# wo in 32 contiguous rows per partition, and head outputs spread by a masked multiply, in a one-core attention block

## The chip, the cores and the metric

The kernel runs on one core of a Trainium2 chip. The metric is the device time of one execution in microseconds. A run over 1.5% above the fastest of its kernel is called slow and is left out of every ratio. Times of one set were taken on the same chip, in turns with the kernel before.

In the profiles, PE is TensorE (PEld its weight loads), DVE is VectorE, ACT is ScalarE, POOL is GpSimd and SP is SyncE, which issues the loads. HBM is the memory in which the inputs stand, SBUF the memory of the core, in 128 partitions. A packet is one piece that a DMA moves, here one run of bytes of a partition; a DMA has landed when its last completion signal is recorded. The granted clock is the share of full speed that the trace gives for TensorE.

## The reference

One decode step: a grouped-query attention over a long cache, times a gate from a small MLP. The attention is cut to what matters here; `xn` is the layer-normed input.

```python
B, Sq, D = 2, 1, 512
Hq, Hkv, Sk, Dh = 32, 8, 32768, 128        # 4 query heads share a KV head
q = (xn @ wq)                              # [B, 32 heads, 128]
scores = einsum("bhqd,bhkd->bhqk", q, k) * Dh**-0.5
o = einsum("bhqk,bhkd->bhqd", softmax(scores), v)
s = o.reshape(B, Sq, Hq * Dh) @ wo         # wo is [4096, 512]
out = x + s * silu(mlp(xn))
```

K and V together are 268 MB. wo is 4 MB and is used last.

## The kernel before

K and V come in 4 MB pieces (one DMA each, 32 KB to every partition) into five buffers that are used in turn. They stand in the pool `slots`, which is laid out behind `pers`, the pool of everything that lives for the whole kernel.

```python
pers = ctx.enter_context(tc.tile_pool(name="pers", bufs=1))
slots = ctx.enter_context(tc.tile_pool(name="slots", bufs=SLOTS))     # 5 x 32 KB per partition
ktp = ctx.enter_context(tc.tile_pool(name="ktp", bufs=T_BUFS))        # transposed keys
# ... other work pools, and PSUM pools
def load_cache(cache, b, g, i, name):
    t = slot(name)
    nc.sync.dma_start(out=t[:, :],
        in_=cache[b, g, i * NK:(i + 1) * NK, :].rearrange("(p t) d -> p (t d)", p=128))
    return t
# ... the parts of pers that the change touches
sel_r = pers.tile([128, NQ, 4, 32], BF16)      # 1024 bytes per partition, filled by 4 copies
mask = pers.tile([128, NQ, rep], F32)          # 64 bytes, filled by 4 reduces
oX = pers.tile([128, Hkv, NQ, B], BF16)
```

At the end of each KV head the head's output is divided by the softmax sum and moved to the partitions where the wo rows lie. Then the last three DMAs, wo, feed 128 output matmuls.

```python
    # end of a head (b, g)
    on = smp.tile([128, rep], BF16, tag="on", name="on")
    nc.vector.tensor_mul(out=on[:, :], in0=oT[:, :], in1=rec[:, :])
    for r in range(NQ):
        nc.tensor.matmul(xp[:, r, :], lhsT=sel_r[:, r, :, :]..., rhs=on[:, :], start=True, stop=True)
    nc.vector.tensor_mul(out=xm[:, :, :], in0=xp[:, :, :], in1=mask[:, :, :])
    nc.vector.tensor_reduce(out=oX[:, g, :, b], in_=xm[:, :, :], axis=AX.X, op=ALU.add)

wo_parts = [(0, 4), (4, 7), (7, 8)]            # of 8 groups, 4 KB per partition each
# ... in the last round, queued behind the last V piece
for a, z in wo_parts:
    nc.sync.dma_start(out=wo3[:, a:z, :], in_=wos[:, a:z, :])
# ... after the loop
for gr in range(Hkv * NQ):
    g, r = divmod(gr, NQ)
    for n in range(NQ):
        c = r * D + n * QW
        nc.tensor.matmul(s_ps[32 * n:32 * n + B, :], lhsT=oX[:, g, r, :], rhs=wo3[:, g, c:c + QW],
                         start=(gr == 0), stop=(gr == Hkv * NQ - 1), tile_position=(0, 32 * n))
# sg = s_ps * g4; out4 = sg + x4; two stores of 1 KB, one by SP, one by ACT
```

The softmax here doesn't subtract the row's maximum and nothing guards it: scores larger than these inputs give would overflow.

## Time and profile before

| what | value | where it is read |
|---|---|---|
| time | 661.57 us | median of 3 runs, 661.44 to 661.58 |
| profiled span | 660.0 us | page |
| bytes moved, mean rate | 280.91 MB, 426 GB/s | page, part 2 |
| PE, DVE busy | 63%, 53% | page, part 1 |
| 32,768 B load packet | 1213 ns (median) | packet records of the trace |
| slowest of the 16 landings of the last wo part | 655.51 us | landing records of the trace |

The page of the kernel before. In part 2 each number is one fortieth of the span; part 4 is the chain of waits followed back from the end; in part 6 the last number is the time from issue to landing.

```profile
span 660.0 us, 6356 instructions
PE 415.5 (63%) x2684; PEld 175.7 (27%) x2684; DVE 347.9 (53%) x442; ACT 50.1 (8%) x152; POOL 6.9 (1%) x20
...
DMA  9999999999999999999999999999999999999995
GB/s 382 419 437 442 418 438 439 424 439 425 434 436 427 439 428 429 440 427 434 437 425 437 432 429 440 425 434 439 427 435 428 435 436 427 437 434 429 432 419 232
...
q1 hardware_dynamic: 10728, 280.50, 98.7%
q8 instruction: 21, 0.34, 0.2%
...
DMA k<-in_A_k_cache_dram 70%; PE sc L304 10%; DVE T L296 7%; DMA wo<-in_A_wo_dram 6%; PE o L336 3%; DVE pt L315 1%; ACT ep L313 0%; PE S L332 0%; PE s_ps L394 0%; DVE sm L331 0%; SPq L93 0%; SPq L380 0%; DVE sg L402 0%; DVE out L404 0%; DVE
...
k<-in_A_k_cache_dram SPq DMA_DIRECT2D x32, 4096.0 KB, 44.9
```

The DMA engines are busy from the first slice to the last, at 418 to 442 GB/s in all slices but the first and the last, and most of the chain is K loads (70%) and wo (6%). A K load lands 44.9 us after its issue, which at 426 GB/s is the time of 4.6 loads of 4.19 MB (an estimate from these numbers), so others are queued ahead of it: the engines do not wait for the core. So the time is the bytes at the rate of the DMA packets, plus what follows the last landing.

The timeline of the end of the kernel before (start, length, engine, line, operation; in brackets the idle time before it and what ended it):

```profile
650.80 0.16 DVE L355 TENSOR_TENSOR on<-oT,rec 128x4 bf16<-128x4 f32 x1 [11.72 <-PE oT L348]
651.02 0.24 PE L358 MATMUL xp<-on,sel_r 128*128 128x4 bf16 x4 [0.25 <-DVE on L355]
651.19 1.06 PE L394 MATMUL s_ps<-wo,oX 128*2 128x128 bf16 x64
651.30 0.17 DVE L363 TENSOR_TENSOR xm<-xp,mask 128x16 f32<-128x16 f32 x1 [0.33 <-PE xp L358]
651.50 0.17 DVE L365 TENSOR_REDUCE oX<-xm 128x4 bf16<-128x16 f32 x1
654.33 1.88 PE L394 MATMUL s_ps<-wo,oX 128*2 128x128 bf16 x64 [2.08 <-DMA wo<-in_A_wo_dram]
656.26 0.29 DVE L402 TENSOR_TENSOR sg<-s_ps,g 98x128 f32<-98x128 f32 x1 [4.58 <-PE s_ps L394]
656.65 0.29 DVE L404 TENSOR_TENSOR out<-sg,x 98x128 bf16<-98x128 f32 x1
656.97 0.65 SPq L406 DMA_DIRECT2D out_dram<-out  x1
```

PE waits 2.08 us for the second wo part, then 64 matmuls fill the time to 656.21. The rest is one multiply, one add and the store.

### The profile page before, as it was taken

To read this page: it belongs to the slowest core of one execution; us is meant where nothing else is said; L and a number is where in the kernel's file an instruction comes from. 1 tells how busy PE (TensorE), PEld (TensorE's weight loads), DVE (VectorE), ACT (ScalarE), POOL (GpSimd) and SP (SyncE) were. 2 spreads that over 40 slices of the span, in tenths; PEclk is the share of its full clock that TensorE was granted. 3 is DMA by queue.
4 is the path that set the end of the run, shared out by engine and by line. 5 is a ranking of instruction groups with operands and counts; after the bars stand their busy time and mean duration, and the time that the engine had idled before them with its cause. 6 is when DMAs were issued, how large, how long until landed. Compare 5 with 4: busy or idle time off the path is not lost.

```text
span 660.0 us, 6356 instructions
## 1 busy us (share of the span) xinstructions
PE 415.5 (63%) x2684; PEld 175.7 (27%) x2684; DVE 347.9 (53%) x442; ACT 50.1 (8%) x152; POOL 6.9 (1%) x20
## 2 busy tenths in 40 slices
PE   2485667565566766467776566766646775656664
PEld 2242223222222322223222122322212232222222
DVE  5563456564445655445656444665644466554450
ACT  1111100000000000000000000000000000000000
POOL 3000000000000000000000000000000000000000
PEclk9985897676888767678777777877778787768886
DMA  9999999999999999999999999999999999999995
GB/s 382 419 437 442 418 438 439 424 439 425 434 436 427 439 428 429 440 427 434 437 425 437 432 429 440 425 434 439 427 435 428 435 436 427 437 434 429 432 419 232
DMA packets 11024, 280.91 MB, mean 426 GB/s; under 512 B 1386, under 2 KB 1396, under 8 KB 2420
## 3 DMA queue, kind: packets, MB, share of 16 engines
q1 hardware_dynamic: 10728, 280.50, 98.7%
q8 instruction: 21, 0.34, 0.2%
q0 software_dynamic: 256, 0.01, 0.0%
q14 instruction: 7, 0.06, 0.0%
q10 hardware_dynamic: 12, 0.00, 0.0%
HBM read 280.50 MB, written 0.00 MB: 425 GB/s over the span
## 4 chain that ended last, share of the span: by engine, by line
DMA 75%; PE 14%; DVE 7%; issue 2%; ACT 0%; SPq 0%; DVEq 0%; ACTq 0%
DMA k<-in_A_k_cache_dram 70%; PE sc L304 10%; DVE T L296 7%; DMA wo<-in_A_wo_dram 6%; PE o L336 3%; DVE pt L315 1%; ACT ep L313 0%; PE S L332 0%; PE s_ps L394 0%; DVE sm L331 0%; SPq L93 0%; SPq L380 0%; DVE sg L402 0%; DVE out L404 0%; DVEq L296 0%
## 5 line engine op out<-in xcount | busy, mean ns | idle before, releaser
L304 PE MATMUL sc<-T,z 128*128 128x512 bf16 x1024 | 301.1, 461 | 179.7 <-DVE T L296 179.5
L296 DVE STREAM_TRANSPOSE T<-k 128x1024 int32<-128x1024 int32 x256 | 292.1, 1207 | 167.7 <-DMA k<-in_A_k_cache_dram 167.7
L304 PEld LDWEIGHTS <-z 128*128 128x128 bf16 x1024 | 114.7, 112 | 365.1 <-issue 283.8
L336 PE MATMUL o<-v,pt 128*16 128x512 bf16 x1024 | 73.8, 439 | 4.9 <-DMA v<-in_A_v_cache_dram 4.9
L315 DVE STREAM_TRANSPOSE pt<-ep 128x512 bf16<-128x512 bf16 x32 | 22.8, 711 | 78.1 <-ACT ep L313 78.1
L313 ACT ACTIVATE ep<-sc 128x512 bf16<-128x512 f32 x32 | 19.1, 597 | 533.5 <-PE sc L304 533.5
L336 PEld LDWEIGHTS <-pt 128*16 128x16 bf16 x1024 | 25.4, 97 | 41.1 <-issue 23.7
L332 PE MATMUL S<-sm,ones_f 128*128 128x4 f32 x64 | 12.1, 260 | 24.8 <-DVE sm L331 24.8
L348 PE MATMUL oT<-sel_o,ob 128*128 128x4 f32 x128 | 16.9, 255 | 11.1 <-ACT ob L345 11.1
L348 PEld LDWEIGHTS oT<-sel_o,ob 128*128 128x128 f32 x128 | 15.5, 191 | 19.4 <-ACT ob L345 19.4
L332 PEld LDWEIGHTS S<-sm,ones_f 128*128 128x128 f32 x64 | 9.7, 191 | 32.5 <-DVE sm L331 32.5
L327 DVE MEMSET o<- 128x512 f32 x16 | 7.8, 485 | 13.4 <-ACT ob L345 12.3
L280 ACT COPY z<-qr 32x16 bf16<-32x16 bf16 x64 | 12.7, 198 | 11.6 <-DVE qr L227 10.9
L355 DVE TENSOR_TENSOR on<-oT,rec 128x4 bf16<-128x4 f32 x16 | 2.6, 161 | 20.2 <-PE oT L348 20.2
L345 ACT COPY ob<-o 128x512 f32<-128x512 f32 x16 | 9.4, 584 | 26.2 <-PE o L336 26.2
L353 DVE RECIPROCAL rec<-S 128x4 f32<-128x4 f32 x16 | 2.9, 182 | 7.3 <-PE S L332 7.2
L358 PEld LDWEIGHTS <-sel_r 128*128 128x128 bf16 x64 | 5.2, 117 | 5.2 <-issue 5.2
L209 PE MATMUL qT_ps<-xT,wq 128*128 128x2 bf16 x128 | 3.6, 165 | 4.5 <-DMA wq<-in_A_wq_dram 4.5
L358 PE MATMUL xp<-on,sel_r 128*128 128x4 bf16 x64 | 3.8, 164 | 4.0 <-DVE on L355 4.0
L313 ACT ACTIVATION_READ_ACCUMULATOR ep<-sc 128x1 f32 x32 | 6.3, 198 | 0.2
L331 DVE TENSOR_SCALAR sm<-sel_h,rs 128x4 f32<-128x4 f32 x32 | 6.0, 188 | 0.0
L363 DVE TENSOR_TENSOR xm<-xp,mask 128x16 f32<-128x16 f32 x16 | 2.8, 174 | 5.3 <-PE xp L358 5.3
(63 smaller groups left out, 48.5 us busy)
## 6 DMA issues: line engine op xcount, KB each, us to landing
k<-in_A_k_cache_dram SPq DMA_DIRECT2D x32, 4096.0 KB, 44.9
v<-in_A_v_cache_dram SPq DMA_DIRECT2D x32, 4096.0 KB, 39.2
wq<-in_A_wq_dram SPq DMA_DIRECT2D x1, 4096.0 KB, 12.5
w<-in_B_w_dram SPq DMA_DIRECT2D x2, 1792.0 KB, 38.0
wo<-in_A_wo_dram SPq DMA_DIRECT2D x1, 2048.0 KB, 34.4
wo<-in_A_wo_dram SPq DMA_DIRECT2D x1, 1536.0 KB, 37.8
wo<-in_A_wo_dram SPq DMA_DIRECT2D x1, 512.0 KB, 38.5
x_bf<-in_A_x_dram POOLq DMA_DIRECT2D x4, 0.5 KB, 9.6
```

The costliest lines, as they stand in the source:

```text
L280: nc.scalar.copy(out=z[32 * j:32 * j + 32, :, :, c:c + rep], in_=qr[32 * j:32 * j + 32, :, :, b, g * rep:(g + 1) * rep],)
L296: nc.vector.transpose(out=T[:, :].rearrange("p (b t k) -> p t b k", b=NB, t=RT), in_=kt[:, r * W:(r + 1) * W].rearrange("p (t b k) -> p t ...
L304: nc.tensor.matmul(sc[:, :], lhsT=z[:, nb, e, zc:zc + 128], rhs=Tb[:, nb, :, e], start=(r == 0 and nb == 0 and e == 0), stop=(r == NR - 1 ...
L313: nc.scalar.activation(out=ep[:, :], in_=sc[:, :], func=ACT.Exp, scale=inv_sqrt_dh, accum_out=rs[:, :])
L315: nc.vector.transpose(out=pt[:, :, :].rearrange("p r (t h) -> p t r h", h=rep), in_=ep[:, :].rearrange("p (t r h) -> p t r h", r=NR, h=rep),)
L327: nc.vector.memset(state["o"][:, :], 0.0)
L331: nc.vector.tensor_scalar_mul(out=sm[:, :], in0=sel_h[:, :], scalar1=rs[:, 0:1])
L332: nc.tensor.matmul(S[:, :], lhsT=ones_f[:, :], rhs=sm[:, :], start=(i == 0), stop=(i == NPART - 1))
L336: nc.tensor.matmul(o[32 * j:32 * j + VT * rep, :], lhsT=pt[:, r, a * VT * rep:(a + 1) * VT * rep], rhs=vt[:, u * VT:(u + 1) * VT, :].rearr ...
L345: nc.scalar.copy(out=ob[:, :], in_=o[:, :])
L348: nc.tensor.matmul(oT[:, :], lhsT=ob[:, t * Dh:(t + 1) * Dh], rhs=sel_o[:, t, :], start=(t == 0), stop=(t == VT - 1),)
L358: nc.tensor.matmul(xp[:, r, :], lhsT=sel_r[:, r, :, :].rearrange("p j w -> p (j w)"), rhs=on[:, :], start=True, stop=True,)
```

## The change

The intent is a shorter end. wo goes to the partitions so that each holds 32 neighbouring rows: a part of `n` rows is then one run of `n` KB per partition. The two big parts have runs of 16 and 12 KB in place of the 4 KB runs before, and the last part can be a single row. The head outputs are brought to that layout by one multiply with a mask per head and a single matmul per batch, in place of four matmuls, a multiply and a reduce per head. The diff is shortened: `...` and what stands in brackets mark cuts.

```diff
+    RW = HD // 128        # 32 rows per partition
+    RQ = Dh // RW         # 4
-    sel_r = pers.tile([128, NQ, 4, 32], BF16)      # filled by 4 copies
+    sel_r = pers.tile([128, RW], BF16)             # filled by one reduce
-    mask = pers.tile([128, NQ, rep], F32)          # filled by 4 reduces
+    mask = pers.tile([128, RQ], F32)               # filled by one reduce
-    oX = pers.tile([128, Hkv, NQ, B], BF16)
+    onx = pers.tile([128, B, Hq, RQ], BF16)
+    oX = pers.tile([128, RW, B], BF16)
     ...
-            on = smp.tile([128, rep], BF16, tag="on", name="on")
+            on = smp.tile([128, rep], F32, tag="on", name="on")
             nc.vector.tensor_mul(out=on[:, :], in0=oT[:, :], in1=rec[:, :])
-            (4 matmuls into xp, one multiply with mask, one reduce into oX[:, g, :, b])
+            nc.vector.tensor_mul(
+                out=onx[:, b, g * rep:(g + 1) * rep, :],
+                in0=on[:, :].unsqueeze(2).to_broadcast([128, rep, RQ]),
+                in1=mask[:, :].unsqueeze(1).to_broadcast([128, rep, RQ]))
+            if g == Hkv - 1:
+                nc.tensor.matmul(xp[:, :], lhsT=onx[:, b, :, :]..., rhs=sel_r[:, :], start=True, stop=True)
+                nc.vector.tensor_copy(out=oX[:, :, b], in_=xp[:, :])
-    wo_parts = [(0, 4), (4, 7), (7, 8)]
+    wo_parts = [(0, RW // 2), (RW // 2, RW - 4), (RW - 4, RW - 1), (RW - 1, RW)]
     ...
-            wos = A_wo.rearrange("(g p r) d -> p g (r d)", p=128, r=NQ)
+            wos = A_wo.rearrange("(p r) d -> p r d", r=RW)
```

The output matmuls stay 128, in the order of the rows.

More of the change, by code (lines that the diff above doesn't have):

```diff
@@ L137 @@
     )
-    sel_r = pers.tile([128, NQ, 4, 32], BF16)
-    for j in range(4):
-        nc.vector.tensor_copy(
-            out=sel_r[:, :, j, :],
-            in_=ident[:, :].rearrange("p (w r) -> p r w", r=NQ),
-        )
-    mask = pers.tile([128, NQ, rep], F32)
-    for r in range(NQ):
+    sel_r = pers.tile([128, RW], BF16)
+    with nc.allow_low_precision(reason="sums of zeros and a single one"):
         nc.vector.tensor_reduce(
-            out=mask[:, r, :],
-            in_=ident[:, :].rearrange("p (h w) -> p h w", h=rep),
+            out=sel_r[:, :],
+            in_=ident[:, :].rearrange("p (q r) -> p r q", r=RW),
             axis=AX.X, op=ALU.add,
         )
+    mask = pers.tile([128, RQ], F32)
+    nc.vector.tensor_reduce(
+        out=mask[:, :],
+        in_=ident[:, :].rearrange("p (q r) -> p q r", r=RW),
+        axis=AX.X, op=ALU.add,
+    )
     zs = [pers.tile([128, NB, 2, ZC], BF16, name=f"z{i}") for i in range(2)]
@@ L353, in emit_v @@
             nc.vector.reciprocal(out=rec[:, :], in_=S[:, :])
-            on = smp.tile([128, rep], BF16, tag="on", name="on")
+            on = smp.tile([128, rep], F32, tag="on", name="on")
             nc.vector.tensor_mul(out=on[:, :], in0=oT[:, :], in1=rec[:, :])
-            xp = f_ps.tile([128, NQ, rep], F32, tag="f", name="xp")
-            for r in range(NQ):
+            nc.vector.tensor_mul(
+                out=onx[:, b, g * rep:(g + 1) * rep, :],
+                in0=on[:, :].unsqueeze(2).to_broadcast([128, rep, RQ]),
+                in1=mask[:, :].unsqueeze(1).to_broadcast([128, rep, RQ]),
+            )
+            if g == Hkv - 1:
+                xp = f_ps.tile([128, RW], F32, tag="f", name="xp")
                 nc.tensor.matmul(
-                    xp[:, r, :], lhsT=sel_r[:, r, :, :].rearrange("p j w -> p (j w)"), rhs=on[:, :],
+                    xp[:, :], lhsT=onx[:, b, :, :].rearrange("p h q -> p (h q)"), rhs=sel_r[:, :],
                     start=True, stop=True,
                 )
-            xm = smp.tile([128, NQ, rep], F32, tag="xm", name="xm")
-            nc.vector.tensor_mul(out=xm[:, :, :], in0=xp[:, :, :], in1=mask[:, :, :])
-            with nc.allow_low_precision(reason="three of the four terms are zero, the fourth is bf16"):
-                nc.vector.tensor_reduce(out=oX[:, g, :, b], in_=xm[:, :, :], axis=AX.X, op=ALU.add)
-    wo_parts = [(0, 4), (4, 7), (7, 8)]
+                nc.vector.tensor_copy(out=oX[:, :, b], in_=xp[:, :])
+    wo_parts = [(0, RW // 2), (RW // 2, RW - 4), (RW - 4, RW - 1), (RW - 1, RW)]
     NW = len(work)
@@ L376 @@
             wo_t = slot("wo")
-            wo3 = wo_t[:, 0:Hq * D].rearrange("p (g c) -> p g c", g=Hkv)
-            wos = A_wo.rearrange("(g p r) d -> p g (r d)", p=128, r=NQ)
+            wo3 = wo_t[:, 0:Hq * D].rearrange("p (r c) -> p r c", r=RW)
+            wos = A_wo.rearrange("(p r) d -> p r d", r=RW)
             for a, z in wo_parts:
@@ L389 @@
     nc.vector.memset(s_ps[:, :], 0.0)
-    for gr in range(Hkv * NQ):
-        g, r = divmod(gr, NQ)
+    for r in range(RW):
         for n in range(NQ):
-            c = r * D + n * QW
             nc.tensor.matmul(
                 s_ps[32 * n:32 * n + B, :],
-                lhsT=oX[:, g, r, :],
-                rhs=wo3[:, g, c:c + QW],
-                start=(gr == 0), stop=(gr == Hkv * NQ - 1),
+                lhsT=oX[:, r, :],
+                rhs=wo3[:, r, n * QW:(n + 1) * QW],
+                start=(r == 0), stop=(r == RW - 1),
                 tile_position=(0, 32 * n),
```

## The prediction

> **What bounds the kernel now.** The loads. The page gives 280.91 MB at a mean 426 GB/s and DMA busy 90% or more in 39 of 40 slices; the chain of waits is 75% DMA. By the trace's packet records a 32,768 B packet takes 1213 ns (median), a 4096 B packet 159 ns: a straight line of 0.0368 ns per byte plus about 8 ns per packet. PE (63% of the span) and DVE (53%) only matter after the last byte.
>
> The landing records show 16 DMA queues that do not finish together: the last wo part lands between 650.69 and 655.51 us. The lag grew over the whole run, in steps of 1.3 to 2 us, each beside a 16,384 B instruction packet (21 of them); the slowest queue took three. [...]
>
> **The tail (timeline).** wo part 1 (rows for groups 0 to 3) lands at 650.49, part 2 at 654.29, part 3 at 655.51. PE does 64 output matmuls from 651.19, waits 2.08 us for part 2, then does the other 64 from 654.33 in 1.88 us with no gap, at granted clock 0.5: 29 ns each. The 48 of part 2 would end at 655.74, after part 3 has landed. So the tail is bound by the landing of part 2, then by PE, not by part 3. Then sg, out and the store: 656.21 to 660.0.
>
> **What the change does.**
> 1. wo: per DMA queue 64 packets of 4096 B (10.18 us) become 8 each of 16, 12, 3 and 1 KB. With the line above: about 611, 460, 121 and 46 ns, 9.9 us. The last byte comes about 0.27 us sooner, 655.25. Rows 28 to 31 stay behind the same second-last big part, so that part lands about 0.36 us sooner, near 653.93.
> 2. A last part of one row leaves 4 matmuls after the last landing in place of 16. Worth nearly nothing here: PE is still busy with the 48 and 12 before it (653.93 + 60 x 29 ns = 655.7, later than 655.25).
> 3. Heads: 64 xp matmuls and their weight loads become 2; the reduce goes, onx comes (about 0.17 us, as xm). All but the last head run under the loads: worth nothing. At the end, on is ready at 650.96; onx, one matmul and one copy bring oX to about 651.8. Every output matmul now waits for it, since the copy writes all 32 rows at once, so the first 64 start near 651.9 rather than 651.19. They take 1.06 to 1.9 us and end by 653.8: inside the old 2.08 us wait, with little to spare.
> 4. Setup (4 copies and 4 reduces fewer) runs under the first loads: nothing. [...] the slowest queue should keep three fetches.
>
> On the critical path: about 0.35 us of 661.57, nearly all from larger packets.
>
> **Prediction: 661.2 us, range 660.6 to 661.8.** Faster by over 2%: 1%; within 2%: 98%; slower: 1%.
>
> **What would show it.** 128 packets each of 16,384, 12,288, 3072 and 1024 B with the times above; the third-last and last wo landings near 653.9 and 655.25; 64 output matmuls back to back after the third part's predecessor lands; span near 659.6; the fast-to-slow spread of landings still about 4.8 us.
>
> **What would make it wrong.** Granted clock 1.0 in the last 4 us (another 0.4 to 0.6 us gained, and point 2 would then count); the first 64 matmuls running past 653.9; a fetch that falls on the slowest queue in the tail (1.3 us), or one fewer there; 1 KB packets costlier than the line says.

A fetch is there, as below, a DMA packet that the trace calls "instruction". The 0.4 to 0.6 us for a granted clock of 1.0 are an estimate. It can be worked out from the same trace: the first 64 output matmuls took 1.06 us (clock 1.0 from 648.73 to 652.15 us), the last 64 took 1.88 us (clock 0.5).

## The result, and the profile after

| | before | after |
|---|---|---|
| time, median of 6 runs each | 661.62 us (661.44 to 661.81) | 665.28 us (665.15 to 665.47) |
| ratio | | 1.0056, 95% interval 1.0043 to 1.0068 |
| profiled span | 660.0 us | 663.4 us |

Here and below, a ratio is the mean time of one kernel's fast runs over the mean of the other's fast runs of the same rounds, so it is not quite the ratio of the medians. The change made the kernel 3.66 us slower by the medians, where 0.35 us faster was predicted.

The page after, the lines that answer to those above:

```profile
span 663.4 us, 6213 instructions
PE 411.3 (62%) x2622; PEld 172.7 (26%) x2622; DVE 344.8 (52%) x422; ACT 50.1 (8%) x152; POOL 7.0 (1%) x20
...
DMA  9999999999999999999999999999999999999994
GB/s 380 419 433 440 428 426 437 427 432 435 422 435 428 431 434 429 430 435 428 433 431 428 433 426 435 432 427 434 427 434 431 424 437 430 425 439 428 429 430 203
...
q1 hardware_dynamic: 10232, 280.50, 98.6%
q8 instruction: 20, 0.33, 0.2%
...
DMA k<-in_A_k_cache_dram 69%; PE sc L307 13%; DMA wo<-in_A_wo_dram 6%; DVE T L299 5%; PE o L339 3%; DVE pt L318 1%; ACT ep L316 0%; PE S L335 0%; PE s_ps L397 0%; DVE sm L334 0%; SPq L95 0%; SPq L385 0%; DVE sg L405 0%; DVE out L407 0%; DVE
...
k<-in_A_k_cache_dram SPq DMA_DIRECT2D x32, 4096.0 KB, 44.3
```

The bound is the same, the bytes on the load queue are the same, and no engine has more to do. The page only says that something general is a little slower. The view that sums a stretch says what. Before, from 100 to 600 us (the last column is the rate, the one ahead of it the DMA share):

```profile
100.00:600.00 500.00, 323.89 (x1838) 131.94 (x1837) 273.58 (x323) 35.18 (x113) 0.00 (x0) 0.78 1.00 432
```

and after:

```profile
100.00:600.00 500.00, 321.07 (x1787) 129.48 (x1786) 271.04 (x310) 34.50 (x111) 0.00 (x0) 0.78 1.00 430
```

The DMA share is 1.00 in both, so the engines did not wait: they were slower at the same work. The loss is in the bulk loads, which the change does not touch.

The timeline of the end, after:

```profile
653.66 0.16 DVE L358 TENSOR_TENSOR on<-oT,rec 128x4 f32<-128x4 f32 x1 [11.54 <-PE oT L351]
653.85 0.17 DVE L359 TENSOR_TENSOR onx<-on,mask 128x16 bf16<-128x16 f32 x1
654.08 0.19 PE L366 MATMUL xp<-sel_r,onx 128*128 128x32 bf16 x1 [0.46 <-DVE onx L359]
654.31 0.20 DVE L370 CAST oX<-xp 128x32 bf16<-128x32 f32 x1 [0.28 <-PE xp L366]
654.56 1.07 PE L397 MATMUL s_ps<-wo,oX 128*2 128x128 bf16 x64 [0.29 <-DVE oX L370]
657.05 1.88 PE L397 MATMUL s_ps<-wo,oX 128*2 128x128 bf16 x64 [1.42 <-DMA wo<-in_A_wo_dram]
658.98 0.29 DVE L405 TENSOR_TENSOR sg<-s_ps,g 98x128 f32<-98x128 f32 x1 [4.48 <-PE s_ps L397]
659.38 0.29 DVE L407 TENSOR_TENSOR out<-sg,x 98x128 bf16<-98x128 f32 x1
659.70 0.66 SPq L409 DMA_DIRECT2D out_dram<-out  x1
```

This end looks as predicted, only 2.7 us late: `sg` starts at 658.98 in place of 656.26, and PE again waits for wo (1.42 us) before the last 64 matmuls.

The packet records of the trace (one record per DMA packet: start, length, bytes) show the difference. This table is counted from them, over the 32,768 B packets that start after 45 us:

| | before | after |
|---|---|---|
| packets counted | 7872 | 7873 |
| exactly 1213 ns | 99.5% | 0.03% |
| 1220 to 1239 ns | 0% | 28% |
| commonest length | 1213 ns | 1216 ns |
| mean | 1214.6 ns | 1219.4 ns |

Every queue is slower from there on. Over all 8320 such packets the means are 1215.86 and 1220.37 ns. Each of the 16 queues takes 520 of them, so an estimate from these means is 520 x 4.51 ns = 2.3 us. The last V piece's slowest landing moved by 2.87 us, from 645.54 to 648.41 us. Part of the rest is that the 16,384 B instruction packets became longer too, with a median of 934 ns before and about 1070 after.

What differs for a K load? Not its issue, its shape or its source. But `sel_r` lost 960 bytes per partition and `mask` 32 (with rounding), and `onx` added 512: `pers` shrank by 480 bytes. In the program as it is built, the first load buffer moved from byte 36,352 of a partition to byte 35,872. The five buffers are 32,768 bytes apart, so all five moved from a multiple of 256 to 32 past one.

There is a second difference in the end. Before, the store's last landing is 1.93 us after its issue (656.97 to 658.90); after, 2.47 us (659.70 to 662.17). In the trace after, an 8192 B instruction packet starts at 660.45, inside the store. Before, the packet of that series came at 617.3 us, and the next one after the store.

**Theory A**: a load buffer that does not start at a multiple of 256 bytes makes every load packet some ns longer. **Rival B**: the instruction stream, shorter by 124 PE instructions, puts the fetches at other times. **Rival C**: the new wo packets or heads do it. **Rival D**: what matters is where the engines' own work tiles stand.

### The profile page after: what moved, and what is told of

Read it like the earlier page. It is cut to its first block, busy times and chain, and to the rows that moved or that the text cites. A ratio compares the mean times of both kernels' runs of the same rounds, so it can differ in the third digit from the quotient of the medians.

```text
span 663.4 us, 6213 instructions
## 1 busy us (share of the span) xinstructions
PE 411.3 (62%) x2622; PEld 172.7 (26%) x2622; DVE 344.8 (52%) x422; ACT 50.1 (8%) x152; POOL 7.0 (1%) x20
## 4 chain that ended last, share of the span: by engine, by line
DMA 75%; PE 16%; DVE 6%; issue 2%; ACT 0%; SPq 0%; DVEq 0%; ACTq 0%
DMA k<-in_A_k_cache_dram 69%; PE sc L307 13%; DMA wo<-in_A_wo_dram 6%; DVE T L299 5%; PE o L339 3%; DVE pt L318 1%; ACT ep L316 0%; PE S L335 0%; PE s_ps L397 0%; DVE sm L334 0%; SPq L95 0%; SPq L385 0%; DVE sg L405 0%; DVE out L407 0%; DVEq L299 0%
## 5 line engine op out<-in xcount | busy, mean ns | idle before, releaser
L358 DVE TENSOR_TENSOR on<-oT,rec 128x4 f32<-128x4 f32 x16 | 2.6, 162 | 20.0 <-PE oT L351 20.0
L212 PEld LDWEIGHTS <-wq 128*128 128x128 bf16 x128 | 3.5, 104 | 4.6 <-DMA wq<-in_A_wq_dram 4.6
L397 PE MATMUL s_ps<-wo,oX 128*2 128x128 bf16 x128 | 3.0, 265 | 1.7 <-DMA wo<-in_A_wo_dram 1.4
```

Of the source, the lines that this page charges most:

```text
L212: nc.tensor.matmul(qT_ps[:, h * B:(h + 1) * B], lhsT=wq3[:, k, h * Dh:(h + 1) * Dh], rhs=xT[:, k, :], start=(k == 0), stop=(k == DK - 1),)
```

## The experiments

The padding in these experiments is an unused tile with one element written once by GpSimd, so that it is allocated. It takes the last place in `pers`, so that only what stands behind it moves. All results were correct.

### Set 1: where the load buffers stand

Changed kernel, buffers moved back to byte 36,352:

```diff
     out4 = pers.tile([128, QW], BF16)
+    pad = pers.tile([128, 240], BF16)       # 480 bytes per partition
+    nc.gpsimd.memset(pad[:, 0:1], 0.0)
```

> The changed kernel with 480 unused bytes after its persistent tiles, so that the five 32 KB load buffers start again at byte 36352 of each partition (a multiple of 256), as in the kernel before, instead of 35872 (32 over a multiple of 256). Theory A (the misaligned buffers make every load packet longer): the 32,768 B packets take 1213 ns again, not 1216 to 1224, and the time is about 661.2 us, 0.35 us under before, as the prediction had it. Rival B (the instruction stream: fewer PE instructions, so that fetches fall at other times) and rival C (the new wo packets or the new heads) leave it near 665.3 us with 1216 ns packets.

Measured: 662.31 us against 661.77 us for before (ratio 1.0009, 0.9995 to 1.0022). The packets are at 1213 ns again, 99.5% of them. So 3.1 of the 3.66 us are gone, and B and C do not cause them. But 0.54 us over before is not 0.35 us under it. Theory A holds for the large part; something else costs about 0.9 us against the prediction.

Kernel before, buffers moved by 32 bytes (the same two lines with `[128, 16]`):

> The kernel before with 32 unused bytes after its persistent tiles: the load buffers start 32 bytes past a multiple of 256, nothing else is changed. Theory A: packets of 1216 to 1224 ns and a time of 664.3 to 665.6 us. Rivals B and C: 661.6 us with packets of 1213 ns, as before.

Measured: 665.10 us (median of five, 664.84 to 665.11 in the four fast runs), ratio 1.0048 (1.0035 to 1.0062). Nothing of the change is in this kernel, and it is as slow as the changed kernel. The remaining run, the profiled one, took 1230.54 us with a slow TensorE; it is a slow run, and it is described under "What stays open".

Kernel before, buffers moved by 128 bytes (`[128, 64]`):

> The kernel before with 128 unused bytes: buffers start 128 past a multiple of 256. If what counts is a multiple of 256, it is as slow as with 32 bytes, 664.3 to 665.6 us; if a multiple of 64 or 128 is enough, 661.6 us. Rivals B and C: 661.6 us.

Measured: 664.47 us, ratio 1.0040 (1.0028 to 1.0053), packets mostly at 1213 to 1221 ns with a mean of 1219.6. A multiple of 128 is not enough.

Kernel before, buffers moved by 256 bytes (`[128, 128]`):

> The kernel before with 256 unused bytes: buffers start at a multiple of 256 that is none of 512. If a multiple of 256 is enough: 661.6 us and packets of 1213 ns. If 512 is needed: 664 to 665.6 us. Rivals B and C: 661.6 us.

Measured: 661.83 us, ratio 0.9999 (0.9987 to 1.0012), packets at 1213 ns. A multiple of 256 that is none of 512 is as good as before.

### Set 2: other tiles, and the rest of the loss

Kernel before, with the padding between the load buffers and the work pools behind them:

```diff
     slots = ctx.enter_context(tc.tile_pool(name="slots", bufs=SLOTS))
+    padp = ctx.enter_context(tc.tile_pool(name="padp", bufs=1))
+    pad = padp.tile([128, 16], BF16)
+    nc.gpsimd.memset(pad[:, 0:1], 0.0)
```

> The kernel before with 32 unused bytes between the load buffers and the tiles that the engines work in (transposed keys, exponentials, small tiles): the load buffers keep their multiple of 256, all work tiles behind them lose it. Theory A (what counts is where a load packet lands): packets of 1213 ns and 661.6 to 661.9 us. Rival D (what counts is where VectorE and TensorE read and write their own tiles): 664.3 to 665.6 us.

Measured: 661.73 us against 661.70 us (ratio 1.0001, 0.9987 to 1.0015), packets at 1213 ns. Rival D falls: what counts is where the load buffers stand. VectorE and TensorE also read these buffers, and their reads moved with them. The record tells the two apart in the tail of the kernel before + 32 (set 4): 23 wo packets start between 656.92 and 657.62 us, while no engine works, and their median is still 162 ns in place of 159. So the longer packets do not need the engines' reads.

For the rest, the traces of the aligned kernels gave two candidates. Here is the end of the aligned changed kernel of set 1:

```profile
652.13 0.20 DVE L370 CAST oX<-xp 128x32 bf16<-128x32 f32 x1 [0.30 <-PE xp L366]
652.38 3.58 PE L397 MATMUL s_ps<-wo,oX 128*2 128x128 bf16 x128 [0.29 <-DVE oX L370]
656.01 0.29 DVE L405 TENSOR_TENSOR sg<-s_ps,g 98x128 f32<-98x128 f32 x1 [3.69 <-PE s_ps L397]
656.41 0.29 DVE L409 TENSOR_TENSOR out<-sg,x 98x128 bf16<-98x128 f32 x1
656.73 0.65 SPq L411 DMA_DIRECT2D out_dram<-out  x1
```

First, in this profile PE runs all 128 output matmuls without a gap, from the moment oX is there: the chain to oX seems to decide (rival F). The granted clock of this execution was 0.5 in the whole tail (from 643.66 us on). When the same kernel was profiled again (set 3), the clock was 1.0 from 648.76 to 652.17 us, oX was there 0.68 us sooner, and PE waited 0.84 us for wo. So a tail without a gap belongs to that execution as much as to the kernel. Second, the store: issued at 656.73, that is 0.24 us earlier than before, it lands last at 658.99, later than before (658.90). Three of ACT's four store packets land by 658.58, the fourth at 658.99; of SP's four, three land by 658.38 and the fourth at 658.81. An 8192 B instruction packet starts at 657.47 (theory E). VectorE has 422 instructions in place of 442, so if the packet is VectorE's, it comes later for that reason.

Aligned kernel with 24 useless VectorE copies near 20 us:

```diff
         in_=qr_ps[:, :, :, :].rearrange("p n e c -> p (n e c)"),
     )
+    junk = pers.tile([128, 16], BF16)
+    for _ in range(24):
+        nc.vector.tensor_copy(out=junk[:, 0:1], in_=qr[:, 0, 0, 0, 0:1])
     ...
-    pad = pers.tile([128, 240], BF16)
+    pad = pers.tile([128, 224], BF16)       # the buffers stay at byte 36352
```

> The changed kernel with aligned load buffers and 24 useless one-element copies on VectorE near 18 to 24 us, where it idles. They bring VectorE's instruction count back to that of before (it lost 20), so its fifth 8 KB instruction fetch should fall near 617 us again, not at 657.5 us in the middle of the output store. Theory E (that fetch delays the last of the store's landings, 658.99 against 658.57 for the rest, and so most of the 0.54 us by which the aligned kernel is over before): 0.4 us less than the aligned kernel, about 661.9 us, the store's four landings within 0.1 us. Rival F (the excess comes from the longer chain to the output matmuls alone): no change, 662.3 us.

Measured: 661.57 us against 661.70 us (ratio 0.9998, 0.9985 to 1.0010). The instruction packet is at 617.27 us again and the store lands 1.84 us after its issue. As theory E had it, but for the size: it gave 0.4 us for the gain, and it is 0.55 us on this chip against the partner run of set 3 (662.12 us).

Aligned kernel with the mask multiplied into the reciprocal:

```diff
-            on = smp.tile([128, rep], F32, tag="on", name="on")
-            nc.vector.tensor_mul(out=on[:, :], in0=oT[:, :], in1=rec[:, :])
+            recm = smp.tile([128, rep, RQ], F32, tag="on", name="recm")
+            nc.vector.tensor_mul(out=recm[:, :, :], in0=rec[:, :]..., in1=mask[:, :]...)   # early
             nc.vector.tensor_mul(
                 out=onx[:, b, g * rep:(g + 1) * rep, :],
-                in0=on[:, :]..., in1=mask[:, :]...)
+                in0=oT[:, :]..., in1=recm[:, :, :])
```

> The changed kernel with aligned load buffers; the reciprocal is multiplied with the mask as soon as it is known, so one VectorE operation instead of two stands between the last oT matmul and the xp matmul. Rival F (in the tail the output matmuls start late, at 652.38 instead of 651.2, and run without a gap to the end, so the chain to oX is on the critical path): 0.2 us less than the aligned kernel, about 662.1 us. If the tail is still bound by the last landings: no change, 662.3 us.

Measured: 662.09 us against 661.70 us (ratio 1.0006, 0.9993 to 1.0018). Its partner on this chip, run in set 3, is 662.12 us, so there is no gain. In its profile PE waits 1.29 us for wo after the first 64 matmuls.

Aligned kernel with the last part of four rows:

```diff
-    wo_parts = [(0, RW // 2), (RW // 2, RW - 4), (RW - 4, RW - 1), (RW - 1, RW)]
+    wo_parts = [(0, RW // 2), (RW // 2, RW - 4), (RW - 4, RW)]
```

> The changed kernel with aligned load buffers and wo in three parts, the last of four rows (rows 28 to 31) in place of three and one. By the prediction's point 2 (a one-row last part is worth nearly nothing, since PE is still busy when it lands): 662.2 to 662.4 us, as the aligned kernel. If the one-row part matters, 12 matmuls at 29 ns more come after the last landing: up to 0.35 us slower.

Measured: 661.96 us against 661.70 us (ratio 1.0004, 0.9991 to 1.0016), and 662.12 us for its partner with the one-row part. The one-row part brings nothing.

### Set 3: the same chip for the pair, a control, and all together

The aligned kernel again:

> The changed kernel with aligned load buffers once more, as the partner on the same chip of the other three runs of this set: 662.3 us, 0.5 us over before.

Measured: 662.12 us against 661.73 us for before (ratio 1.0006, 0.9994 to 1.0019).

The kernel with the 24 VectorE copies again:

> The aligned kernel with 24 useless VectorE copies once more, now on the same chip as the aligned kernel. Theory E (VectorE's fifth instruction fetch hits the output store): 661.6 us, 0.5 to 0.7 us under the aligned kernel. If the two earlier values differed because of their chips: 662.3 us.

Measured: 661.64 us (ratio 0.9997, 0.9985 to 1.0010), 0.48 us under the aligned kernel on the same chip. The runs reach from 661.08 to 661.86 us; the aligned kernel's from 661.88 to 662.42.

The same 24 copies on GpSimd (`nc.gpsimd.tensor_copy` in place of `nc.vector.tensor_copy`):

> The same 24 useless copies on GpSimd, so that VectorE's instruction count stays at the changed kernel's. Theory E: VectorE's fetch stays near 657.5 us and the time at 662.3 us, as the aligned kernel. If the copies help in another way (by the moment at which they run): 661.6 us.

Measured: 662.32 us (ratio 1.0012, 0.9998 to 1.0025). The instruction packet stays at 657.5 us, the store takes 2.25 us, and the time stays high. So it is VectorE's instruction count that moves this packet, and the packet goes with the 0.5 us. The intervals of the ratios are too wide for 0.5 us, but the single runs on this chip hardly overlap: 15 of kernels with the VectorE copies take 661.08 to 661.86 us (median 661.59), 20 of aligned kernels without them 661.80 to 662.90 us (median 662.1).

Aligned, VectorE copies and short chain together (the two edits above in one kernel):

> The changed kernel with aligned load buffers, the 24 useless VectorE copies and the short chain: the candidate to beat both kernels. The prediction's 661.2 us, 0.35 us under before, should appear here if its terms were right and only the two layout effects were missed; 661.6 us or more if the larger wo packets gain nothing.

Measured: 661.65 us against 661.73 us (ratio 0.9999, 0.9986 to 1.0011). It does not beat the kernel before by anything that these intervals can tell, and rival F falls again: the short chain adds nothing to 661.64 us. (Its profile too fell in an execution at clock 0.5, and PE again runs all 128 output matmuls without a gap, from 652.46 us: the short chain does not remove that picture.)

### Set 4: the packets at 32 and 64 bytes

The 32-byte offset again, for a profile in a fast execution:

> The kernel before with load buffers 32 bytes past a multiple of 256, once more, since its only profile fell in an execution of 1230 us in which TensorE was slow. Theory A: 665 us again, and in a fast profile the 32,768 B packets at 1216 to 1224 ns like the changed kernel's, the 4096 B packets of wo some 3 to 4 ns over 159.

Measured: 665.19 us against 661.80 us (ratio 1.0051, 1.0036 to 1.0066). The lengths of its load packets are those of the changed kernel nearly to the packet:

| length of a 32,768 B packet | changed kernel | before, buffers + 32 |
|---|---|---|
| 1216 ns | 4411 | 4413 |
| 1224 ns | 1731 | 1733 |
| 1215 ns | 756 | 757 |
| 1221 ns | 500 | 497 |
| 1213 ns | 340 | 344 |

The view that sums 100 to 600 us gives this kernel the 430 GB/s of the changed one:

```profile
100.00:600.00 500.00, 319.09 (x1835) 130.70 (x1835) 273.05 (x322) 34.50 (x111) 0.00 (x0) 0.78 1.00 430
```

and the aligned changed kernel of set 1 the 432 GB/s of before:

```profile
100.00:600.00 500.00, 309.82 (x1771) 128.67 (x1800) 272.03 (x313) 35.17 (x113) 0.00 (x0) 0.80 1.00 432
```

The 4096 B packets of wo have a median of 162 ns in place of 159. By the means they take 3.8 ns more (159.5 to 163.3), where the packets eight times as long take 4.9 ns more (1214.6 to 1219.5). So the cost is nearer to one per packet than to one per byte. It is not a constant either: in the changed kernel against its aligned copy the wo packets of 16,384, 12,288 and 3072 B take 4.6, 5.3 and 3.3 ns more in the mean, but those of 1024 B, the last to move, only 0.3 ns.

The kernel before with buffers moved by 64 bytes (`[128, 32]`):

> The kernel before with load buffers 64 bytes past a multiple of 256. If only a multiple of 256 is enough, 664.3 to 665.2 us, like the offsets 32 and 128; if a multiple of 64 did, 661.7 us, and the slow offset of 128 would be unexplained.

Measured: 664.49 us (ratio 1.0041, 1.0024 to 1.0058). Of the offsets tried, only a multiple of 256 is free:

| first load buffer, bytes past a multiple of 256 | kernel | time | its own before |
|---|---|---|---|
| 0 | before + 256 | 661.83 us | 661.77 us |
| 32 | before + 32 | 665.10, 665.19 us | 661.77, 661.80 us |
| 32 | after | 665.28 us | 661.62 us |
| 64 | before + 64 | 664.49 us | 661.80 us |
| 128 | before + 128 | 664.47 us | 661.77 us |
| 0 | after + 480 | 662.31, 662.12 us | 661.77, 661.73 us |

So there is no cost at a multiple of 256 (661.83 us against 661.77 at + 256), a cost at 32, 64 and 128 bytes past one (3.3 to 3.4, 2.7 and 2.7 us), and one that grows little with the length of the packet (3.8 ns for 4096 B, 4.9 ns for 32,768 B). It is the SBUF side of a load, where it writes, whose alignment was changed; the HBM side stayed. What happens within a packet is not shown.

### What stays open

Some features of the records are not explained. In the misaligned kernels, the load packets up to about 32 us mostly still take 1213 ns (in the changed kernel 337 of the 357 that start between 4 and 32 us, and none of the 109 between 40 and 48 us), and the longer lengths set in queue by queue between 22 and 41 us, in the same buffers. In the slow execution of the kernel before + 32 the buffers are misaligned too, but its loads pause (the loads' packets fill 56% of the DMA engines' time), and after the first 120 us hardly any packet takes 1216 or 1224 ns, while 5999 of the 8320 take 1213 and the wo packets have a median of 159. That is one slow execution and no experiment. Nothing here tells why the longer lengths set in late. And at offset 32, where 1216 ns is the rule, the 1224 ns packets of a queue mostly come four packets apart, if each load is counted as its eight data packets and one semaphore packet. Why is open, and so is why offset 32 costs more (3.4 us) than 64 and 128 (2.7 us).

That the instruction packet at 657.5 us slows the store is inferred, and how it would is open. Shown are the coincidence (five profiles of four kernels with the packet between the store's issue and its landing, and 2.25 us or more between these two) and its absence (with the 24 VectorE copies). In the aligned kernel the record of that packet ends at 657.89 us, before the first store packet starts at 657.98, and what comes 0.4 us late is the last landing of each of the two stores. The short chain, told below, does not fit in.

The slow execution itself is open too. It is the only one of the 68 timed executions of variants (three chips) that took 1230.54 us in place of 665, with the DMA no longer the bound. In its profile the matmuls of 512 columns took a mean of 1089 ns, where they take 461 in the kernel before; its mean clock is given as 1.0, and its page has no line of granted clock. Three lines of its page:

```profile
span 1228.7 us, 6326 instructions
...
PE   3999999999999989999999999989999999999997
...
L304 PE MATMUL sc<-T,z 128*128 128x512 bf16 x992 | 822.1, 1089 | 42.2 <-DVE T L296 23.1
```

## Why the prediction was wrong

The predicted sum was "about 0.35 us of 661.57, nearly all from larger packets". The medians give +3.66 us. Point by point:

1. **Bound: right.** The DMA share is 1.00 in the bulk of both kernels. This is also why a few ns per packet show at once in the time.
2. **wo packets: right in kind, a little too large in size.** In the aligned kernel the packets have medians of 611, 460, 121 and 46 ns, exactly the line's values. From the last V piece's slowest landing to the last wo landing, three kernels with the old parts and aligned buffers (before, + 256, and work tiles + 32) take 9.97, 9.95 and 9.92 us; the aligned changed kernel and its copy in set 3 take 9.76 and 9.70, and no other aligned variant of the changed kernel more than 9.79. That is 0.2 us where 0.27 was predicted, and about as much for the second-last big part (0.36 predicted).
3. **The one-row last part: right, worth nothing** (661.96 against 662.12 us without and with it).
4. **Heads: right that they cost nothing that the times show.** After, the first 64 output matmuls come 6.15 us after the last V landing in place of 5.65, and PE still waits 1.42 us for wo. In the profiles of executions at clock 0.5 the wait was used up (aligned kernel of set 1; all together), as the prediction's "little to spare" feared, but a shorter chain gained nothing in the times (662.09 against 662.12 us, 661.65 against 661.64).
5. **The step that failed** is in point 4 of the prediction, "Setup (4 copies and 4 reduces fewer) runs under the first loads: nothing", and with it the sum on the critical path, which left the K and V packets as they were. (By the diff it is six instructions fewer, since two reduces are new; the time of these instructions was not the matter.) Setup has sizes too. With `onx` its tiles shrank by 480 bytes per partition, all five load buffers lost their multiple of 256, and the load packets went from 1213 to mostly 1216 and 1224 ns: 3.1 to 3.4 us, shown both ways, by padding the changed kernel (from +3.66 us over its own before to +0.54 and +0.39) and by misplacing the kernel before (+3.33 and +3.39 us).
6. **A second term was missing, of about 0.5 us**: 20 fewer VectorE instructions moved an 8192 B instruction packet into the output store (aligned 662.12 us, fetch moved 661.64 us on one chip). The prediction counted PE's fetches, not VectorE's, and looked for them on the slowest load queue, not on the store's. (The 16,384 B packets, q8 on the page, are put down to PE by their number: 21 before, with 2684 matmuls and as many weight loads, and 20 after, with 2622.) Whether an engine waits for a fetch in the body of this kernel was not looked at. But a fetch takes time from one DMA queue (before, the first one, of 948 ns, stands between two load packets, and the one after it took 1685 ns in place of 1213), and the one that fell into the store went with 0.5 us.

The store, read from the landing records (issue to the last landing), shows point 6 in one table:

| kernel | VectorE's late instruction packet | issue to last landing |
|---|---|---|
| before + 256; before, work tiles + 32 | 617 us | 1.84, 1.84 us |
| aligned; aligned again; four-row part; copies on GpSimd | 657 us | 2.26, 2.27, 2.27, 2.25 us |
| aligned, fetch moved; again; all together | 616 to 618 us | 1.84, 1.85, 1.85 us |
| after | 660.5 us | 2.47 us |

The kernels not in the table have no such packet in the store and take 1.85 us (before + 128) to 1.93 us (before, before + 32).

The short chain is an exception. It has the packet at 657.5 us, but its store takes 1.86 us; instead VectorE stands still for 0.47 us ahead of its last operation:

```profile
656.04 0.29 DVE L409 TENSOR_TENSOR sg<-s_ps,g 98x128 f32<-98x128 f32 x1 [4.72 <-PE s_ps L401]
656.80 0.29 DVE L413 TENSOR_TENSOR out<-sg,x 98x128 bf16<-98x128 f32 x1 [0.47 <-DVE sg L409]
```

The time lost is about the same, and the time of the kernel too. Why it falls there is open.

Together: against its own before, the changed kernel is at +3.66 us; aligned, at +0.54 and +0.39; with the fetch moved as well, at -0.13 and -0.09. The gain that the change was made for is seen in the packet records, 0.2 us between the last V and the last wo landing. In the times it is those 0.13 and 0.09 us, which these intervals of about 0.13% (0.9 us) cannot tell from nothing.

## What to carry to other kernels

When a kernel is bound by its loads, print the SBUF addresses of the load buffers before and after any change to tile sizes, however small the tile: here 480 bytes of setup tables outweighed the whole intended gain by ten times. Start large DMA destinations at a multiple of 256 bytes (here 32, 64 and 128 bytes past one cost 3.3 to 3.4, 2.7 and 2.7 us of 662), by padding as here (putting their pool first was not tried). And before believing a difference of half a microsecond, look whether an instruction fetch has moved into the last store (here one went with 0.4 us more from the store's issue to its last landing and about 0.5 us in the time).
